# Attention, then two feed-forward stages: one unit's weights of each iteration copied into a rounded-format tile, transpositions moved to the end of the iteration two later

## The chip, the cores and the metric

The kernel runs on one core of a Trainium2 chip. That core has TensorE (PE in the profile; PEld is its weight load), VectorE (DVE), ScalarE (ACT), GpSimd (POOL) and SyncE (SP), which here only issues transfers. Each engine works through its own list of instructions in order and waits on semaphores that others raise. The metric is the device time of one execution in microseconds. The kernel before takes a median of 922.79 us over 3 runs (922.45 to 923.26).

## The reference

```python
def _attn_ref(q, k, v, tau):                      # q, k, v: 4 batches x 8 heads x 576 x 64
    scores = scale * np.matmul(q, k.transpose(0, 1, 3, 2))
    thresh = np.max(scores, axis=-1, keepdims=True) - tau
    scores = np.where(scores >= thresh, scores, -1000000000.0)
    scores = scores - np.max(scores, axis=-1, keepdims=True)
    attn = np.exp(scores)
    attn = attn / (np.sum(attn, axis=-1, keepdims=True) + 1e-09)
    return np.matmul(attn, v)
def reference(**kwargs):
    attn_out = _attn_ref(...)                      # -> x: 2304 tokens x 512
    x = _moe_ref(x=x, ...)                         # router, then one of 8 experts a token: relu(x w1) w2
    return _moe2_ref(x=x, ...)                     # h = x w_in; (h * sigmoid(1.702 h)) w_out
```

The change is in the attention. A row of the scores keeps only the entries within tau of its maximum; the exponentials of these, the weights, are summed and multiplied with the values.

## The kernel before, in words

Attention works on 16 pairs of heads of one batch. A pair is cut into 9 units: unit w = 2c + h (w under 8) has 128 queries of head h against all 576 keys, and unit 8 has the last 64 queries of both heads. That makes 144 units, taken two at a time in 72 iterations; an iteration's place in the pattern is k = it % 9, since nine iterations are two pairs of heads. Two tables indexed by k, AV and ROW, say how many items of value matmuls and of rows an iteration takes off their queues; AVL and ROWL do so for the last iterations. The loop is `run`.

In an iteration each engine is given, in this order of the program:

- scores (`qk`, L227), 6 matmuls a unit, 12 for unit 8. Queries and keys were each split into a rounded part and a rest (tiles qkh and qkl, format fp32r) by GpSimd (`split`, L149 to L151), so that three matmuls in that format give the product. They go into 4 banks that two units share by turns (ring).
- transpositions (`trans`, L313): four of 128 x 128 of the weights E of each of the two units of the iteration ahead, into one of three accumulators named tr, which rows and tails use too, in turn. ScalarE copies each accumulator into AT (L315, L317). In iterations k = 0, 2, 5, 7 come the transpositions of the last 64 keys, called tails (`trans_tails`, L331 to L335), copied to ATt (L340).
- per unit the negated maximum on VectorE (`max`, L255) and the exponential on ScalarE (`exp`, L261); behind these the copies of the transposed weights; then per unit the mask and sum on VectorE (`mask`, L285), which writes E (or ET for unit 8).
- value matmuls (`av_items`, L357), five items for each half of a pair, the last of them with the tails (L363) and a ScalarE copy to xT (L364).
- rows (`row_items`, L397): xT back to tokens by a matmul with G, which also gives the router's logits; copied by ScalarE to xr (L402), scaled by GpSimd (L405, L410), stored to DRAM by SP (L416).
- one or two items of GpSimd's splitting, and small steps of the router (`sides`; L658 adds a bias on VectorE).

F holds a pair's queries and keys, V its values; SP loads them two or three pairs ahead (L124, L128).

## Time and profile before

| what | us |
|---|---|
| median of 3 runs | 922.79 |
| profiled execution | 921.75 |
| its span | 920.0 |
| PE, DVE, ACT, POOL busy in the span | 898.1, 510.3, 445.2, 233.2 |
| attention, from the first scores to the first matmul of the next stage | 5.69 to 306.68 |
| nine iterations in the steady part (145.88 to 181.23) | 35.35 |

Busy time is what the instructions of an engine cover together. Matmuls overlap each other and their loads, so a mean duration of 280 ns for a small matmul isn't its share of the path; what a run of matmuls costs is read from the chain of waits, where pieces follow each other without overlap. The stretches of nine iterations below begin at the scores with k = 0.

### The profile page before, as it was taken

The numbers are of one execution on the slowest core, as the hardware profiler recorded it, in microseconds if no ns is written. First come the engines' busy times: TensorE is split into PE (matmuls) and PEld (weight loads), VectorE is DVE, ScalarE is ACT, GpSimd is POOL, SyncE is SP. The second block draws the span as 40 slices with busy tenths as digits, with TensorE's granted clock in tenths as the row PEclk, the third lists the DMA queues.
The fourth block names the chain that finished last, engine by engine and source line by source line (L and its number), as shares of the span: only waits on it lengthen the run. The fifth ranks groups of instructions, "written<-read, shape, count | busy, mean of one in ns | idle before, by whom it ended". The sixth has DMA issues, their size and how long they took to land.

```text
span 920.0 us, 14322 instructions
## 1 busy us (share of the span) xinstructions
PE 898.1 (98%) x5341; PEld 716.4 (78%) x5341; DVE 510.3 (55%) x1104; ACT 445.2 (48%) x787; POOL 233.2 (25%) x333
## 2 busy tenths in 40 slices
PE   9999999999999999999999999999999999999994
PEld 7677776776766788878889888888888888888894
DVE  7888889889787574678787588611111121111110
ACT  6777777777776533555545455422222222222221
POOL 7845655556544501010610000010001000100100
PEclk9999999999999999999999999999999999999997
DMA  7213432242102735465756153310001000100100
GB/s 257 73 46 122 140 128 72 71 131 74 36 9 76 239 103 187 142 230 178 229 183 231 68 184 117 112 46 12 24 12 46 7 12 7 46 0 1 46 1 26
DMA packets 53756, 85.67 MB, mean 93 GB/s; under 512 B 9300, under 2 KB 35058, under 8 KB 53682
## 3 DMA queue, kind: packets, MB, share of 16 engines
q1 hardware_dynamic: 50098, 74.63, 25.0%
q0 software_dynamic: 3312, 9.94, 3.3%
q8 instruction: 44, 0.72, 0.3%
q14 instruction: 30, 0.25, 0.1%
q10 hardware_dynamic: 272, 0.13, 0.0%
HBM read 67.57 MB, written 17.11 MB: 92 GB/s over the span
## 4 chain that ended last, share of the span: by engine, by line
PE 81%; DVE 7%; issue 6%; ACT 2%; DMA 2%; POOL 1%; SPq 0%; POOLq 0%; ACTq 0%
PE tr L1033 29%; PE sc L1058 19%; PE sc L1077 9%; PE sc L227 7%; PE av L357 6%; PE tr L313 6%; DVE E L285 3%; PE tr L397 2%; PE av L363 2%; DVE e L255 2%; ACT e L261 1%; DMA cv_raw<-in_moe_w_in_dram 1%; DMA xg<-y_first 1%; DVE bl L1303 1%; PE av L1005 1%
## 5 line engine op out<-in xcount | busy, mean ns | idle before, releaser
L1270 DVE TENSOR_TENSOR hl<-sg,hh 128x512 fp32r<-128x512 f32 (+1 forms) x80 | 51.1, 638 | 261.5 <-ACT hh L1268 259.1
L1267 ACT ACTIVATE sg<-tr 128x512 f32<-128x512 f32 (+1 forms) x80 | 44.3, 554 | 226.9 <-PE tr L1033 226.9
L261 ACT ACTIVATE e<-e,thr 128x576 f32<-128x576 f32 x144 | 109.6, 776 | 75.2 <-DVE e L255 74.6
L255 DVE TENSOR_SCALAR_CACHE_REDUCE e<-sc,taue 128x576 f32<-128x576 f32 x144 | 112.8, 815 | 33.7 <-PE sc L227 33.3
L1058 PE MATMUL sc<-wo_h,hh 128*128 128x512 f32 x288 | 112.2, 390 | 0.0
L1058 PE MATMUL sc<-wo_l,hh 128*128 128x512 f32 x288 | 112.2, 390 | 0.0
L1058 PE MATMUL sc<-wo_h,hl 128*128 128x512 f32 x288 | 112.0, 389 | 0.0
L285 DVE SCALAR_TENSOR_TENSOR E<-sc,thr,e 128x576 f32<-128x576 f32 x128 | 100.4, 813 | 5.1 <-ACT e L261 4.4
L1033 PE MATMUL tr<-xl,wi_h 128*128 128x512 f32 (+1 forms) x320 | 78.7, 368 | 0.0
L1033 PE MATMUL tr<-xh,wi_l 128*128 128x512 f32 (+1 forms) x320 | 78.7, 368 | 0.0
L1033 PE MATMUL tr<-xh,wi_h 128*128 128x512 f32 (+1 forms) x320 | 78.6, 368 | 0.0
L357 PE MATMUL av<-AT,V 128*64 128x288 f32 x512 | 77.3, 420 | 1.1 <-DVE ixs L933 0.6
L313 PE MATMUL tr<-ident,E 128*128 128x128 f32 x512 | 71.2, 279 | 0.0
L315 ACT COPY AT<-tr 128x512 f32<-128x512 f32 x128 | 68.2, 577 | 0.0
L1033 PEld LDWEIGHTS tr<-xh,wi_h 128*128 128x128 f32 x320 | 57.7, 188 | 11.1
L1033 PEld LDWEIGHTS tr<-xh,wi_l 128*128 128x128 f32 x320 | 56.9, 189 | 10.0
L1033 PEld LDWEIGHTS tr<-xl,wi_h 128*128 128x128 f32 x320 | 56.9, 189 | 9.9
L151 POOL TENSOR_TENSOR qkl<-F,qkh 128x640 fp32r<-128x640 f32 (+1 forms) x30 | 63.1, 2102 | 2.5
L313 PEld LDWEIGHTS tr<-ident,E 128*128 128x128 f32 x512 | 55.1, 141 | 10.3 <-issue 8.7
L1058 PEld LDWEIGHTS sc<-wo_h,hl 128*128 128x128 f32 x288 | 54.1, 188 | 11.3
L227 PE MATMUL sc<-qkh 64*128 64x288 f32 x320 | 57.0, 353 | 6.0 <-DVE E L285 4.2
L1058 PEld LDWEIGHTS sc<-wo_h,hh 128*128 128x128 f32 x288 | 54.1, 188 | 10.7
(262 smaller groups left out, 1578.2 us busy)
## 6 DMA issues: line engine op xcount, KB each, us to landing
F<-in_kq_dram SPq DMA_DIRECT2D x15, 896.0 KB
ra<-in_moe_w_dram SPq DMA_DIRECT2D x20, 512.0 KB
rb<-in_moe_w_dram SPq DMA_DIRECT2D x20, 512.0 KB
cv_raw<-in_moe_w_in_dram SPq DMA_DIRECT2D x16, 512.0 KB
cv_raw<-in_moe_w_out_dram SPq DMA_DIRECT2D x16, 512.0 KB
V<-in_vp_dram SPq DMA_DIRECT2D x16, 320.0 KB
x_dram<-xrow SPq DMA_DIRECT2D x72, 64.0 KB
y_rest<-blank SPq DMA_DIRECT2D x8, 256.0 KB
```

Source lines behind the costliest of these rows:

```text
L151: nc.gpsimd.tensor_sub(lo, x, hi.bitcast(F32))
L227: m = nc.tensor.matmul(self.banks[:, bank, 0:288], a[rs, q:q + 128], b[rs, k:k + 288], start=(n == 0), stop=(n == len(ops) - 1),).ins
L255: self.read(u, nc.vector.tensor_scalar(e, d["sc", w], self.taue[:, 0:1], 3.0e38, op0=ALU.add, op1=ALU.min, accum_out=thr))
L261: self.nc.scalar.activation(d["e", w], d["e", w], ACTF.Exp, bias=d["thr", w][:, 0:1], scale=-1.0)
L285: self.read(u, nc.vector.scalar_tensor_tensor(out=E.rearrange("p (a c) -> p a c", a=2), in0=d["sc", w], scalar=d["thr", w][:, 0:1], in1=d[ ...
L313: nc.tensor.transpose(tp[:, kc * 128:(kc + 1) * 128], E[:, k0 + kc * 128:k0 + (kc + 1) * 128], self.ident)
L315: return lambda: nc.scalar.copy(AT[:, h, :, c * 128:(c + 1) * 128], tp.rearrange("p (k c) -> p k c", k=4))
L357: nc.tensor.matmul(d["av"][h * 64:(h + 1) * 64, 0:288], d["V"][:, h, kc, :], d["AT"][:, h, kc, cols], start=(kc == 0), stop=False, skip_gr ...
L1033: nc.tensor.matmul(hps[:, 0:T], w[:, kd, :], blk[x][:, kd, 0:T], start=(i == 0), stop=(i == 11))
L1058: nc.tensor.matmul(y, h[:, cs], w, start=(f == 0 and i == 0), stop=(f == blk["nf"] - 1 and i == 2))
L1077: nc.tensor.matmul(blk["y"][d], w[:, ds], h[:, 0:T], start=(f == 0 and i == 0), stop=(f == last and i == 2))
L1270: return [upper, lambda: nc.vector.tensor_sub(hl, sg, hh.bitcast(F32))]
```

## The change

Each iteration's first unit gets a copy of its 512 columns of weights: `lay` has SP copy E into a tile R of the rounded format (bits are kept, the tile's type is fp32r), behind that unit's mask. `trans` transposes R with an identity of that type if there is an R, and E as before otherwise. Transpositions no longer follow the scores of the next iteration; they stand at the end of the iteration two later, behind value matmuls and rows, and their ScalarE copies stand there too. ATt is taken from its pool with the first tails instead of with the first transposition. E has five buffers instead of four, F two instead of three.

`split` takes queries by head, so it has three steps in place of two, and the loads of F come in two halves that are queued among these steps. Stores of rows to DRAM are collected and issued behind the masks of the next iteration. The tables AV, ROW, AVL, ROWL and FILL (matmuls on the identity in the first iterations) have other numbers. The router's small sum always takes a tr accumulator.

```diff
--- before.py
+++ after.py
@@ -25,12 +25,12 @@
 UPP = 9
 PJ = 9
 QW, KW = 1280, 640
-AV = (2, 2, 3, 3, 2, 2, 3, 2, 1)
+AV = (1, 3, 2, 3, 2, 2, 3, 2, 2)
 TURNS = ((0, 1), (2, 3))
 TAILS = {2: -1, 5: -2, 7: -2, 0: -1}
 IT_LAST = (NPAIR - HP) * UPP // 2
-AVL = (2, 2, 3, 2, 3, 2, 3, 2, 1, 2, 2, 3, 3, 2, 2, 3, 3, 2, 5)
-ROWL = (0, 1, 0, 1, 1, 1, 1, 1, 1, 0, 0, 0, 0, 1, 0, 1, 0, 1, 0)
+AVL = (1, 3, 2, 3, 2, 2, 3, 2, 2, 1, 3, 2, 3, 2, 2, 3, 2, 2, 1, 5)
+ROWL = (2, 0, 1, 0, 0, 1, 1, 1, 1, 1, 0, 0, 0, 0, 0, 0, 1, 0, 1, 1)
 NS0 = 7
 CA = (0, 1, 2, 2, 2, 2, 2, 2, 2, 2, 2, 2, 2, 2, 2, 2)
 CB = (0, 0, 0, 1, 0, 1, 0, 1, 0, 1, 0, 1, 0, 0, 0, 0)
@@ -40,12 +40,12 @@
 NBW = 6
 F0 = (0, 1, 0)
 NROW = 2
-FILL = (14, 12, 12, 12, 4)
+FILL = (14, 16, 12, 12, 6)
 SN = 1
 SD = (1, 2, 2, 2, 1)
 TAU_MAX = 104.0
 W_TOP = (1.875 - 2.0 ** -23) * 2.0 ** -96
-ROW = (0, 1, 0, 1, 1, 0, 1, 0, 1)
+ROW = (2, 0, 1, 0, 0, 0, 0, 1, 1)
 
 class Attention:
 
@@ -74,8 +74,9 @@
         self.banks = P("a_sc", 1, space=PSUM).tile([128, 4, 512], F32, name="sc")
         Q = lambda name, bufs: late_ctx.enter_context(tc.tile_pool(name=name, bufs=bufs, side="right"))
         cst = P("a_const", 1)
-        self.fp = P("a_f", 3)
-        self.ep = P("a_e", 4)
+        self.fp = P("a_f", 2)
+        self.er = P("a_er", 3)
+        self.ep = P("a_e", 5)
         self.ex = P("a_exp", 3)
         self.et = P("a_et", 2)
         self.sm = P("a_small", 4)
@@ -89,6 +90,8 @@
         self.rp = Q("a_rows", 2)
         self.rw = Q("a_xrow", 6)
 
+        self.idr = cst.tile([128, 128], F32R, name="idr")
+        nc.gpsimd.tensor_copy(self.idr, ident)
         self.cq = cst.tile([128, 1], F32, name="cq")
         self.taue = cst.tile([128, 1], F32, name="taue")
         self.tau = tau
@@ -118,10 +121,13 @@
                 )
 
 
-    def load(self, p):
-        d = self.st[p] = {}
-        d["F"] = F = self.fp.tile([128, KW + 2 * S], F32, name="F")
-        self.nc.sync.dma_start(F, self.kq[p])
+    def load(self, p, parts=(0, 1)):
+        if 0 in parts:
+            self.st[p] = {"F": self.fp.tile([128, KW + 2 * S], F32, name="F")}
+        n = (KW + 2 * S) // 2
+        for i in parts:
+            cs = slice(i * n, (i + 1) * n)
+            self.nc.sync.dma_start(self.st[p]["F"][:, cs], self.kq[p][:, cs])
 
     def load_v(self, p):
         V = self.vp.tile([128, 640], F32, name="V")
@@ -142,7 +148,9 @@
     def split(self, p, i):
 
         nc = self.nc
-        x, (hi, lo) = (self.keys, self.queries)[i](p)
+        x, (hi, lo) = self.queries(p) if i else self.keys(p)
+        if i:
+            x, hi, lo = (t[:, i - 1] for t in (x, hi, lo))
         if i == 0 and p == 1:
             nc.scalar.activation(x, x, ACTF.Copy, scale=self.cq[:, 0:1])
         elif i == 0:
@@ -296,6 +304,16 @@
             ]
 
 
+    def lay(self, u):
+
+        p, w = divmod(u, UPP)
+        d = self.st[p]
+        c, h = divmod(w, 2)
+        E = d["E", 4] if w == 8 else d["E", c][:, h]
+        k0 = 64 if w < 8 and h == 1 else 0
+        d["R", w] = self.er.tile([128, 512], F32R, name="R")
+        self.nc.sync.dma_start(d["R", w].bitcast(F32), E[:, k0:k0 + 512])
+
     def trans(self, u):
 
         nc = self.nc
@@ -304,13 +322,17 @@
         c, h = divmod(w, 2)
         if w == 0:
             d["AT"] = self.at.tile([128, 2, 4, S], F32, name="AT")
-            d["ATt"] = self.at.tile([128, S], F32, name="ATt")
-        AT, ATt = d["AT"], d["ATt"]
+        AT = d["AT"]
         tp = self.ps_tr.tile([128, 512], F32, name="tr")
+        R = d.pop(("R", w), None)
         E = d["E", 4] if w == 8 else d["E", c][:, h]
         k0 = 64 if w < 8 and h == 1 else 0
         for kc in range(4):
-            nc.tensor.transpose(tp[:, kc * 128:(kc + 1) * 128], E[:, k0 + kc * 128:k0 + (kc + 1) * 128], self.ident)
+            cs = slice(kc * 128, (kc + 1) * 128)
+            if R is not None:
+                nc.tensor.transpose(tp[:, cs].bitcast(F32R), R[:, cs], self.idr)
+            else:
+                nc.tensor.transpose(tp[:, cs], E[:, k0 + kc * 128:k0 + (kc + 1) * 128], self.ident)
         if w < 8:
             return lambda: nc.scalar.copy(
                 AT[:, h, :, c * 128:(c + 1) * 128], tp.rearrange("p (k c) -> p k c", k=4))
@@ -323,6 +345,8 @@
         nc = self.nc
         p, w = divmod(u, UPP)
         d = self.st[p]
+        if w == 3:
+            d["ATt"] = self.at.tile([128, S], F32, name="ATt")
         ATt = d["ATt"]
         c0 = 0 if w == 3 else 2
         n = 256
@@ -413,7 +437,8 @@
                 rr.unsqueeze(3).broadcast_to([w, 2, 2, 64]),
             )
             for u in range(2 if kc < 4 else 1):
-                nc.sync.dma_start(xd[b, 2 * kc + u][:, hh * 256:(hh + 1) * 256], xrow[u * 64:(u + 1) * 64, :])
+                self.stores.append(lambda u=u: nc.sync.dma_start(
+                    xd[b, 2 * kc + u][:, hh * 256:(hh + 1) * 256], xrow[u * 64:(u + 1) * 64, :]))
             if hh == 1 and kc == 4:
                 items, gate = self.router.gate_items(b, lgt)
                 self.side.extend([None] * (1 if b == B - 2 else NROW) + items + self.router.after_batch(b, gate))
@@ -428,27 +453,29 @@
         rest = self.first()
         self.load_v(0)
         self.load_v(1)
-        self.load(2)
-        self.poolq = []
+        self.poolq, self.stores = [], []
         self.avq, self.rowq, self.side = avq, rowq, side = [], [], []
         side += [None] * NS0 + [self.gate_setup, *self.router.setup_items(self.setup), *self.extra]
         it = done = 0
         while done < NU:
             last = it >= IT_LAST
             us = [u for u in (2 * it, 2 * it + 1) if u < NU]
-            ts = [u for u in (2 * it - 2, 2 * it - 1) if 0 <= u < NU]
+            ts = [u for u in (2 * it - 4, 2 * it - 3) if 0 <= u < NU]
             starts = [u // UPP for u in us if u % UPP == 0]
             for p in starts:
-                if p + 3 < NPAIR:
-                    self.load(p + 3)
-                if p + 2 < NPAIR:
+                if 0 < p < NPAIR - 2:
                     self.load_v(p + 2)
                 for n in range(1 if p == 0 else p + 2, min(p + 3, NPAIR)):
                     self.poolq += [lambda n=n, i=i: self.split(n, i) for i in range(2)]
+                    if n + 2 < NPAIR:
+                        self.poolq += [lambda n=n: (self.split(n, 2), self.load(n + 2, (0,)))]
+                        self.poolq += [lambda n=n: self.load(n + 2, (1,))]
+                    else:
+                        self.poolq += [lambda n=n: self.split(n, 2)]
             k = it % 9
             for u in us:
                 self.qk(u)
-            copies = [self.trans(u) for u in ts]
+            copies = []
             if it > 1 and k in TAILS:
                 copies.append(self.trans_tails(2 * it + TAILS[k]))
             for i in range(2):
@@ -461,12 +488,18 @@
                 c()
             while rest:
                 rest.pop(0)()
+            if it == 0:
+                self.load(2)
+                self.load_v(2)
             if self.norm:
                 self.norm.pop(0)()
             for i, u in enumerate(us):
                 self.mask(u)
+                if i == 0:
+                    self.lay(u)
                 if last:
                     self.sides(SD[i + 2], False)
+            self.store()
             if it < len(FILL) and FILL[it]:
                 warm = self.ps_av.tile([128, 512], F32, name="av")
                 for _ in range(FILL[it]):
@@ -477,6 +510,8 @@
             while m and rowq:
                 rowq.pop(0)()
                 m -= 1
+            for c in [self.trans(u) for u in ts]:
+                c()
             n = 1 if it else 2
             while n and self.poolq:
                 self.poolq.pop(0)()
@@ -489,12 +524,18 @@
                     avq += self.av_items(p, w // 8)
             it += 1
 
+    def store(self):
+
+        while self.stores:
+            self.stores.pop(0)()
+
     def tail(self, n):
 
         for _ in range(n):
             for q in (self.avq, self.rowq):
                 if q:
                     q.pop(0)()
+                    self.store()
                     break
         return bool(self.avq or self.rowq)
 
@@ -918,7 +959,7 @@
 
         def sum_up(c0, c1):
             if c0 == 0:
-                t["ip"] = self.ps_av.tile([128, 512], F32, name="av") if first else self.ps_tr.tile([128, 512], F32, name="tr")
+                t["ip"] = self.ps_tr.tile([128, 512], F32, name="tr")
             for c in range(c0, c1):
                 nc.tensor.matmul(
                     t["ip"][:, 0:2 * nh], OL[:, c, :], R[:, c].rearrange("p i h -> p (i h)"),
```

TensorE in an iteration with k = 0 (the 36th, counted from 0), before, from behind its scores to the first scores of the next; E and ET are weights, tr the accumulators, G the matrix that turns rows:

```order
L313 MATMUL tr<-ident,E 128x128 [waits Activation_49]
L313 MATMUL tr<-ident,E 128x128 x3
L313 MATMUL tr<-ident,ET 128x128 [waits Activation_49]
L313 MATMUL tr<-ident,ET 128x128 x3
L331 MATMUL tr<-ident,ET 128x128 [waits Activation_49]
L332 MATMUL tr<-ident,ET 64x128
L335 MATMUL tr<-ident,E 128x128 x2
L357 MATMUL av<-AT,V 64x288 x2
L363 MATMUL av<-ATt,V 128x288
L227 MATMUL sc<-qkh_139 128x288 [waits DVE_49]
```

The same iteration after, from behind its scores:

```order
L355 MATMUL tr<-ident,ET 128x128 [waits Activation_49]
L356 MATMUL tr<-ident,ET 64x128
L359 MATMUL tr<-ident,E 128x128 x2
L387 MATMUL av<-ATt,V 128x288
L421 MATMUL tr<-G,xT 128x144 [waits Activation_49]
L421 MATMUL tr<-G,xT 128x144
L421 MATMUL tr<-G,xT 128x144 [waits Activation_49]
L421 MATMUL tr<-G,xT 128x144
L333 MATMUL tr<-idr,R 128x128 [waits DMAHW0_49,Activation_49]
L333 MATMUL tr<-idr,R 128x128 x3
L335 MATMUL tr<-ident,E 128x128 [waits Activation_49]
L335 MATMUL tr<-ident,E 128x128 x3
```

The eight transpositions moved behind the tails, the tail value (L387) and now two rows (L421); the value matmuls on AT are in other iterations, and the last four transpositions wait for ScalarE.

ScalarE in the same iteration, before; e is the exponential, AT and ATt the transposed weights:

```order
L261 ACTIVATE e<-e,thr 128x576 [waits DVE_49,Activation_49] x2
L315 COPY AT<-tr 128x4x128 [waits PE_49]
L317 COPY AT<-tr 128x4x2x64 [waits PE_49]
L340 COPY ATt<-tr 128x320 [waits PE_49]
L364 COPY xT<-av 128x288 [waits PE_49]
L261 ACTIVATE e<-e,thr 128x576 [waits DVE_49,Activation_49] x2
```

After:

```order
L269 ACTIVATE e<-e,thr 128x576 [waits DVE_49,Activation_49] x2
L364 COPY ATt<-tr 128x320 [waits PE_49]
L388 COPY xT<-av 128x288 [waits PE_49]
L426 COPY xr<-tr 128x288 [waits PE_49,Pool_49]
L426 COPY xr<-tr 128x288 [waits PE_49,Activation_49,Pool_49]
L337 COPY AT<-tr 128x4x128 [waits PE_49] x2
L269 ACTIVATE e<-e,thr 128x576 [waits DVE_49]
```

The copies of AT moved from right behind the exponentials to the end of the iteration, behind the copies of ATt, xT and the rows.

## Rows read from the trace of the kernel before

**Rows 1.** Stretches of nine iterations: from:to, length; busy (instructions) by engine; clock; DMA.
```profile
5.69:38.50 32.81, 30.88 (x277) 23.99 (x277) 28.73 (x72) 23.45 (x41) 29.26 (x32) 1.00 0.39 149
38.50:73.75 35.25, 34.71 (x290) 24.16 (x290) 30.09 (x81) 26.09 (x48) 19.08 (x32) 1.00 0.26 82
...
109.36:145.88 36.52, 35.33 (x297) 25.14 (x296) 31.53 (x80) 26.29 (x50) 19.88 (x21) 1.00 0.30 96
145.88:181.23 35.35, 35.30 (x298) 25.17 (x298) 30.25 (x83) 26.51 (x51) 20.42 (x24) 1.00 0.29 89
...
254.93:288.33 33.40, 32.16 (x278) 22.45 (x277) 30.24 (x88) 24.20 (x48) 17.21 (x57) 1.00 0.06 12
288.33:306.68 18.35, 17.20 (x131) 12.35 (x129) 9.41 (x20) 10.76 (x23) 9.20 (x17) 1.00 0.65 199
```

**Rows 2.** One iteration, k = 7, in the same view.
```profile
173.83:177.18 3.35, 3.35 (x31) 2.38 (x31) 2.48 (x7) 2.22 (x5) 3.19 (x6) 1.00 0.00 0
```

**Rows 3.** Chain of waits, 145.8 to 181.3: start us, us, what.
```profile
161.72 1.39 PE sc L227 x18
...
164.12 0.64 PE av L357 x4
...
165.93 0.98 PE sc L227 x12
166.91 1.02 PE tr L313 x8
...
168.16 0.22 PE tr L335 x2
168.38 1.12 PE av L357 x8
...
172.73 0.68 PE av L363 x2
173.41 0.49 PE tr L397 x4
...
176.27 1.57 DVE E L285 x4
...
180.61 0.69 PE tr L397 x4
```

**Rows 4.** Groups by line and shape: x count, busy us, mean ns, idle before.
```profile
L1033 PE MATMUL tr<-xl,wi_h 128*128 128x512 f32 x256 | 68.4, 389 | 0.0
...
L1033 PEld LDWEIGHTS tr<-xh,wi_h 128*128 128x128 f32 x320 | 57.7, 188 | 11.1
...
L1033 PE MATMUL tr<-xl,wi_h 128*128 128x256 f32 x64 | 10.3, 283 | 0.0
```

**Rows 5.** Timeline, ScalarE, in k = 0: start us, us, what.
```profile
147.51 1.51 ACT L261 ACTIVATE e<-e,thr 128x576 f32<-128x576 f32 x2 [0.91 <-DVE e L255]
...
149.40 0.59 ACT L317 COPY AT<-tr 128x512 f32<-128x512 f32 x1
149.87 0.44 ACT L340 COPY ATt<-tr 128x320 f32<-128x320 f32 x1
150.19 0.42 ACT L364 COPY xT<-av 128x288 f32<-128x288 f32 x1
```

**Rows 6.** Timeline, all engines, 241.3 to 243; in brackets idle time and releaser.
```profile
241.43 0.56 ACT L317 COPY AT<-tr 128x512 f32<-128x512 f32 x1
...
242.05 0.54 PEld L397 LDWEIGHTS tr<-G,xT 128*128 128x128 f32 x4 [0.54 <-ACT AT L317]
```

**Rows 7.** Timeline of GpSimd and VectorE around 137; durations of L658.
```profile
136.57 2.65 POOL L151 TENSOR_TENSOR qkl<-F,qkh 128x1152 fp32r<-128x1152 f32 x1
...
137.09 2.18 DVE L658 TENSOR_TENSOR L<-L,bias 128x40 f32<-128x40 f32 x1
...
L658 DVE TENSOR_TENSOR L<-L,bias x4: 189/1192/2184, 137.1 to 315.0; 128x40 f32<-128x40 f32 x4
```

**Rows 8.** Half a microsecond of the transfer of V, in stretches.
```profile
59.50:60.00 0.50, 0.50 (x6) 0.50 (x7) 0.50 (x3) 0.00 (x0) 0.50 (x2) 1.00 0.82 302
```

## The prediction

> **What bounds the kernel now.** I read the stretches of nine iterations first (they show how much of the span the attention takes and whether it is even), then the chain of waits inside one such stretch, then the rows of single operations on it. Attention runs from 5.69 us to the first matmul of the second stage at 306.68 us; the steady stretch takes 35.35 us, and TensorE is busy for 35.30 of them, VectorE for 30.25, ScalarE for 26.51, at a granted clock of 1.00, the 2.4 GHz level [rows 1]. So in the steady state TensorE is the bound. One iteration of the nine isn't: the seventh (k = 7, counting k from 0) takes 3.35 us [rows 2], and the chain there leaves TensorE for two masks, 1.57 us of VectorE, before the next scores [rows 3]. 3.35 is therefore my floor for an iteration: scores, maxima, exponentials, masks and the scores again run in a ring over the same banks, and no change to transpositions shortens that.
>
> The prices on TensorE's path come from the chain [rows 3]: scores 0.98 (1.39 with a unit of tails), eight transpositions 1.02, two tail transpositions 0.22 (so 0.11 each, and 1.02 is 8 x 0.11 with 0.14 of edge), value matmuls 0.64 for one item and 1.12 for two (0.16 + 0.48 an item), the tail value 0.68, a row 0.49 behind a tail value and 0.69 behind value matmuls.
>
> **The change part by part.**
>
> *The format.* Half of the transpositions, 4 of 8 in an iteration and 288 in all, now read a rounded-format tile. No row shows that operation. Lower bound: the same format costs 389 ns at 512 columns and 283 at 256, so 0.053 us per 128 columns when nothing but columns counts [rows 4]. Upper bound with no harm: F32's 0.11. Beyond that it could be worse, since a weight load in the rounded format lasts 188 ns by itself [rows 4] and might not hide behind a short matmul; taken wholly unhidden that is 0.19. The nearest row is the scores: 12 matmuls of that format, each with its own load of 128 columns, in 0.98 us, or 0.082 each [rows 3]. I take 0.08. The difference of 0.03 is worth 36 x 0.03 = 1.1 us in nine iterations, if nothing else ends later.
>
> A rule of the Trainium skill speaks against this, TensorE: Matmul & The Clock Gate, section LDWEIGHTS (loading the stationary operand): a load takes the number of columns over 1.2 in ns, whatever the rest. For 128 columns that would be an estimated 107 ns in either format, and the format would gain nothing (the third case below). The 0.98 for 12 loads of 128 columns speaks against it, though those loads fill only half of the rows each.
>
> *The order.* The group of eight stands behind the value matmuls and rows now, in front of the next scores, instead of behind the scores. By the same edges it costs 4 x 0.08 + 4 x 0.11 + 0.14 = 0.90 behind value matmuls and 0.76 behind a row or tail value, which as the chain shows begin without the edge. Four of the nine are of the first kind, five of the second: 4 x 0.90 + 5 x 0.76 = 7.4 against 9 x 1.02 = 9.2. Together with one more 0.16 saved (eight starts of value matmuls, not nine), TensorE's work falls by 2.0 us per nine iterations, format included.
>
> *The waits that it adds.* Three accumulators serve all of these transpositions and the rows in turn. In an iteration with tails the tails take one, a row another, and the fourth allocation needs the first again. It is freed by ScalarE's copy, and ScalarE makes the copies only behind both exponentials, which end at 147.51 + 1.51 = 149.02, 3.14 us after the scores of that iteration began, at 145.88 [rows 1, 5]. That TensorE does wait so is in the trace once already: a row's load sat 0.54 us for the copy of AT and began 0.06 behind its end, 241.43 + 0.56 = 241.99 [rows 6]. A copy begins about 0.12 before the one ahead of it ends (149.40 + 0.59 against 149.87).
> - k = 0: work 0.98 + 0.44 + 0.68 + 0.49 + about 0.45 + 0.76 = 3.80. But the last four transpositions wait for the first row's copy, which stands behind ATt (0.44) and xT (0.42) on ScalarE: 3.14 + 0.44 + 0.42 + about 0.41 - 3 x 0.12 = 4.05, then 0.06 and 4 x 0.11 = 4.55, with an edge 4.65. Cost 0.85.
> - k = 2 and 7: work 3.77 each; the last four wait for the ATt copy, about 3.14 + 0.44 - 0.12 + 0.06 + 0.44 = 3.96, with an edge 4.0. Cost 0.25 each.
> - k = 4: work 1.39 + 0.64 + 0.68 + 0.76 = 3.47, under the ring, 3.35 + 0.41 for the longer scores = 3.7. Cost 0.2.
> - k = 5: work 3.44, with the ring of the iteration ahead about 3.75. Cost 0.3.
> - k = 1 and 3: 0.98 + 1.60 + 0.90 = 3.48; k = 6: 3.54; k = 8: 3.96. No wait.
> That is 4.65 + 2 x 4.0 + 3.7 + 3.75 + 6.96 + 3.54 + 3.96 = 34.56; I take 34.85, since the ring makes each edge of 0.03 to 0.05 late that I left out. So of the 2.0 us, 1.5 is given back, and 0.5 is left of each steady stretch.
>
> *Two stretches with a blocked VectorE.* At 137.09 a small addition takes 2.18 us while GpSimd's subtraction of 1152 columns (2.65 us) is under way; its fastest case takes 0.19 [rows 7]. The stretch around it takes 36.52, 1.17 more than the steady one [rows 1], and a later one is like it. Now the queries are split by head, so the subtraction is 576 wide, an estimated 1.4 us, and by its place should end ahead of that addition. I take -1.0 for each of the two; at worst 0.
>
> *Start and end.* The first stretch is GpSimd's (29.26 busy of 32.81 [rows 1]): 0. In the second no rows stand in k = 0 and 2 yet, so those waits are absent and it gains nearly the whole 2.0: -1.9. The eighth (33.40) runs by the end's own tables: I take -1.0. The drain of 18.35 [rows 1] gets one iteration more: the last units are transposed two later, and their copy must land first. That adds the group and the copy's time that the remaining values don't cover: +2.5 (0.76 at least, 4 at most).
>
> *Transfers.* 72 copies of 256 KB on SP's queue. The transfer of V reached 302 GB/s [rows 8], so a copy alone needs an estimated 1 us and its fixed time; it is issued behind the first mask, some 3.3 us into an iteration, and read some 7 us later. What stands behind it on SP, the stores and loads, has more time than that. In steady state 0. At the start, copies stand behind the loads of the third pair: +0.5 (0 to 2).
>
> The sum: 0 - 1.9 - 5 x 0.5 - 2 x 1.0 - 1.0 + 2.5 + 0.5 = -4.4 us. The profiled execution took 921.75, of which 920.0 span, and lies 1.04 under the median 922.79; the difference carries over, so the forecast is 922.8 - 4.4 = 918.4.
>
> **The rivals.** They hang on the price of a rounded transposition, since all else is the same. 288 of them, and about half of a change in price arrives, because k = 0, 2, 4, 5 and 7 end on waits.
> - *The price is the lower bound, 0.053.* The columns alone count and the load hides, as for 512 columns. 288 x 0.027 = 7.8, half 3.9: 914.5. For it: every long matmul of that format hides its 188 ns. Against: the scores' 0.082.
> - *The format gains nothing, 0.11.* 288 x 0.03 = 8.6, half 4.3: 922.7. For it: a load of 188 ns is no shorter than any F32 load. The gain of order and of GpSimd is then eaten by the waits at k = 0, 2, 7 and by the drain.
> - *Slower: the load is not hidden.* The place is the four rounded transpositions of each iteration; it decides above 0.11 each. At 0.14 nothing is absorbed any longer: 922.7 + 288 x 0.03 = 931; with 0.125, 927. For it: 188 ns by itself and a moving side of 128 columns only. Against: the scores.
> - *The copies are late.* If a copy takes beyond 7 us from the mask, TensorE stands in every iteration: 0.1 us is 7 us in all, 925. Against: 89 GB/s in the steady stretch [rows 1] against 302 reached.
>
> **How the numbers follow.** Forecast 0.42 (own range 916.4 to 920.8, from the bounds of the drain and of the blocked stretches); lower price 0.22; no gain 0.17; load not hidden 0.10; late copies 0.09. The range 914.5 to 926 leaves out half of the last two and the far end of the second. A measurement of this kernel tells 0.2%, 1.8 us, from no change: faster than that is the forecast, less a tenth of it, and the second case, 0.60; the third gives most of the 0.2 of no change; slower 0.20.
>
> **What would show it.** Right: rounded transpositions 0.08 apart; a wait of TensorE for a ScalarE copy of a row in every k = 0 and of ATt in k = 2 and 7; steady stretches of 34.6 to 35.1; the router's addition back near 0.2; a drain of 20 to 21. Wrong: waits on the copy's DMA outside the first iterations and the end; a steady stretch under 34.3 (the price is lower, or the waits are not there) or above 35.4.

## The result and the profile after

The changed kernel took 927.39 us (median of 4 runs, 926.05 to 928.01) against 922.62 for the kernel before (4 runs): 1.0051 times as long, 95% interval 1.0039 to 1.0063. So it is 4.8 us slower, where 4.4 us faster was forecast and 926 was the upper end of the range.

The busy times on the page of the profiled execution, whose span is 926.2 us:

```profile
PE 896.1 (97%) x5347; PEld 711.3 (77%) x5347; DVE 511.6 (55%) x1104; ACT 449.4 (49%) x787; POOL 239.4 (26%) x364
```

TensorE does less (896.1 us instead of 898.1) in a span that is 6.2 us longer; the time is in waits. The stretches of nine iterations again, which answer to [rows 1]; the last line is the drain to the first matmul of the next stage. The last two lines are divided one iteration later than in [rows 1], so only their sum can be compared:

```profile
5.68:39.07 33.39, 31.04 (x279) 23.71 (x278) 29.13 (x73) 23.03 (x39) 29.65 (x42) 1.00 0.63 213
39.07:74.26 35.19, 33.42 (x285) 22.84 (x285) 31.19 (x81) 25.97 (x47) 17.68 (x29) 1.00 0.43 141
74.26:110.20 35.94, 34.82 (x297) 24.25 (x297) 29.32 (x77) 26.90 (x50) 22.45 (x28) 1.00 0.65 214
110.20:146.33 36.13, 35.16 (x297) 24.38 (x296) 30.34 (x81) 27.03 (x50) 20.56 (x26) 1.00 0.59 191
146.33:183.32 36.99, 35.34 (x297) 24.39 (x296) 32.08 (x82) 27.17 (x51) 21.36 (x31) 1.00 0.48 149
183.32:219.58 36.26, 35.24 (x297) 24.34 (x297) 31.49 (x84) 27.02 (x50) 20.71 (x27) 1.00 0.48 153
219.58:257.30 37.72, 35.85 (x305) 25.33 (x305) 30.09 (x85) 27.85 (x53) 23.17 (x36) 1.00 0.33 105
257.30:293.83 36.53, 34.10 (x303) 23.37 (x302) 32.56 (x95) 26.16 (x50) 17.50 (x57) 1.00 0.23 77
293.83:311.39 17.56, 15.62 (x111) 12.00 (x111) 6.94 (x14) 10.37 (x23) 10.57 (x19) 1.00 0.75 233
```

That stage begins at 311.39 instead of 306.68, 4.7 us later. Against the steps of the prediction: the first stretch was forecast at 32.8 (and 0.5 for the start) and took 33.4; the second at 33.3 and took 35.2; the five behind it, 181.2 us before, at 176.7 and took 183.0; the last stretch and the drain together, 51.8 before, at 53.3 and took 54.1. Nearly the whole miss, 8.2 of 9.1 us, is in the second to seventh stretch.

One of these, iteration by iteration, k = 0 to 8 (length, then busy time by engine):

```profile
110.20:114.90 4.70, 4.32 (x37) 3.51 (x36) 3.53 (x11) 3.86 (x9) 1.26 (x4) 1.00 0.93 276
114.90:118.71 3.81, 3.59 (x34) 2.36 (x34) 3.04 (x8) 2.89 (x6) 3.66 (x6) 1.00 0.79 290
118.71:123.29 4.58, 4.50 (x33) 2.75 (x34) 3.90 (x11) 3.25 (x7) 3.85 (x5) 1.00 0.35 106
123.29:126.81 3.52, 3.52 (x33) 2.35 (x32) 2.81 (x8) 2.58 (x5) 3.28 (x5) 1.00 0.38 130
126.81:130.62 3.81, 3.54 (x33) 2.56 (x33) 3.01 (x9) 2.50 (x6) 3.66 (x4) 1.00 0.88 268
130.62:134.50 3.88, 3.88 (x33) 2.53 (x33) 3.71 (x10) 2.76 (x7) 3.72 (x4) 1.00 0.60 210
134.50:138.32 3.82, 3.81 (x31) 2.46 (x30) 3.65 (x10) 3.21 (x7) 0.21 (x1) 1.00 0.20 73
138.32:142.37 4.05, 4.05 (x36) 2.85 (x35) 3.46 (x12) 3.14 (x7) 0.22 (x2) 1.00 0.58 178
142.37:146.33 3.96, 3.96 (x39) 3.00 (x38) 3.21 (x8) 2.84 (x6) 0.71 (x3) 1.00 0.57 182
```

| k | 0 | 1 | 2 | 3 | 4 | 5 | 6 | 7 | 8 |
|---|---|---|---|---|---|---|---|---|---|
| forecast | 4.65 | 3.48 | 4.0 | 3.48 | 3.7 | 3.75 | 3.54 | 4.0 | 3.96 |
| measured | 4.70 | 3.81 | 4.58 | 3.52 | 3.81 | 3.88 | 3.82 | 4.05 | 3.96 |

Six of nine are within 0.13. k = 1, 2 and 6 are off by 0.3 to 0.6, and VectorE is behind all three. For k = 1 and 2, the timeline from 115.89 to 119.45:

```profile
115.89 1.89 POOL L157 TENSOR_SCALAR F<-F,cq 128x640 f32<-128x640 f32 x1
...
117.19 0.60 DVE L301 COPY rs<-rsT 64x2 f32<-64x2 f32 x1
...
118.71 0.40 PE L235 MATMUL sc<-qkh 64*128 64x288 f32 x2 [0.22 <-DVE E L293]
...
119.44 0.19 PEld L235 LDWEIGHTS sc<-qkh 64*128 64x128 f32 x2 [0.31 <-DVE E L293]
```

The copy of 64 x 2 numbers at L301, a step of the normalisation that `run` places in front of the masks, took 0.60 us; it began while GpSimd scaled 640 columns (115.89 + 1.89 = 117.78) and ended at 117.79. Undisturbed it takes 0.16, and both masks behind it came late by the difference; the next scores waited 0.22 us for the first mask, and those of the second unit 0.31 for the second. The light iteration had no TensorE work left to cover that. In k = 6 the second unit's scores waited 0.24 for the second mask of k = 5, whose maxima had begun behind a router step of 0.78 us (L697).

The price of the rounded transposition, though, is as forecast. Chain of waits (start, us, what), behind value matmuls, then behind a tail value:

```profile
133.64 0.47 PE tr L333 x4
134.11 0.46 PE tr L335 x4
...
137.63 0.30 PE tr L333 x4
137.93 0.47 PE tr L335 x4
...
139.40 0.37 PE tr L359 x2
```

Four rounded transpositions take 0.30 us, 0.075 each (forecast 0.08), and the four in F32 behind them 0.46. The group costs 0.93 behind value matmuls and 0.76 to 0.77 behind a tail value (forecast 0.90 and 0.76). What I left out is the edge of 0.15 that moved to the tails: 0.37 for two tail transpositions right behind scores, where they were 0.22 behind other transpositions [rows 3].

The wait that was forecast for k = 0 is there, for the copy of ATt and then the row's:

```profile
113.71 0.53 PE L333 MATMUL tr<-idr,R 128*128 128x128 f32 x4 [0.31 <-ACT ATt L364]
...
114.31 0.42 PEld L335 LDWEIGHTS tr<-ident,E 128*128 128x128 f32 x4 [0.21 <-ACT xr L426]
```

And the router's addition of [rows 7] is short again, as forecast, min/median/max:

```profile
L699 DVE TENSOR_TENSOR L<-L,bias x4: 193/195/202, 135.0 to 319.7; 128x40 f32<-128x40 f32 x4
```

But other small steps now meet GpSimd's. VectorE and GpSimd around 157:

```profile
157.08 1.40 POOL L159 TENSOR_TENSOR qkl<-F,qkh 128x576 fp32r<-128x576 f32 x1
...
157.09 1.42 DVE L302 TENSOR_SCALAR r<-rs 128x20 f32<-128x20 f32 x1
```

L302, 20 numbers a partition, lasts 1.42 us, to the end of GpSimd's subtraction (157.08 + 1.40 = 158.48). The shorter subtraction did not end these meetings; it moved them. The Trainium skill, SBUF — State Buffer, section "SBUF: two separate sides", says that the port pair which VectorE and GpSimd share is "an exclusive lock, not a bandwidth split". The ends of the two agree within 0.03 us here.

This meeting cost little: k = 2 and 3 of its stretch take 4.58 and 3.68, where the stretch above has 4.58 and 3.52. Another one, of a router step in k = 4 of the same stretch, cost more; its durations (min/median/max), and k = 4 and 5:

```profile
L719 DVE TENSOR_TENSOR oh<-v,valid x4: 194/200/1403, 167.5 to 321.1; 128x40 bf16<-128x40 f32 x4
...
163.17:168.82 5.65, 5.37 (x51) 3.86 (x50) 4.82 (x13) 3.50 (x7) 5.08 (x6) 1.00 0.89 282
168.82:171.42 2.60, 2.11 (x18) 1.24 (x18) 2.43 (x8) 1.70 (x3) 2.40 (x5) 1.00 0.26 93
```

Together these two take 8.25, 0.56 more than the 3.81 and 3.88 above. In the second stretch L667, 1.5 us at 58.3, does the same: k = 4 and 5 take 5.93 and 2.43 there.

### The profile page after: what moved, and what is told of

Read it like the earlier page. It is cut to its first block, busy times and chain, and to the rows that moved or that the text cites. A ratio compares the mean times of both kernels' runs of the same rounds, so it can differ in the third digit from the quotient of the medians.

```text
span 926.2 us, 14670 instructions
## 1 busy us (share of the span) xinstructions
PE 896.1 (97%) x5347; PEld 711.3 (77%) x5347; DVE 511.6 (55%) x1104; ACT 449.4 (49%) x787; POOL 239.4 (26%) x364
## 4 chain that ended last, share of the span: by engine, by line
PE 73%; issue 8%; DVE 6%; DMA 5%; POOL 4%; ACT 3%; SPq 0%; POOLq 0%; ACTq 0%; DVEq 0%
PE tr L1074 27%; PE sc L1099 19%; PE sc L1118 7%; PE sc L235 6%; PE av L381 5%; PE tr L335 2%; DMA cv_raw<-in_moe_w_in_dram 2%; PE tr L421 2%; DVE E L293 2%; PE tr L333 2%; DVE e L263 1%; POOL qkl L159 1%; DMA R<-E 1%; PE av L387 1%; ACT e L269 1%
## 5 line engine op out<-in xcount | busy, mean ns | idle before, releaser
L337 ACT COPY AT<-tr 128x512 f32<-128x512 f32 x128 | 70.4, 593 | 2.1 <-PE tr L333 1.4
L159 POOL TENSOR_TENSOR qkl<-F,qkh 128x576 fp32r<-128x576 f32 (+1 forms) x45 | 65.8, 1462 | 3.7
L1099 PEld LDWEIGHTS sc<-wo_h,hl 128*128 128x128 f32 x288 | 54.1, 188 | 11.4
L1099 PEld LDWEIGHTS sc<-wo_h,hh 128*128 128x128 f32 x288 | 54.1, 188 | 10.6
L1099 PEld LDWEIGHTS sc<-wo_l,hh 128*128 128x128 f32 x288 | 54.1, 188 | 10.6
L1363 POOL DMA_INDIRECT out_dram<-cv_e,iscA x4 | 4.0, 993 | 223.5 <-ACT cv_e L1433 222.9
```

What stands on the lines that cost most here:

```text
L159: nc.gpsimd.tensor_sub(lo, x, hi.bitcast(F32))
L337: return lambda: nc.scalar.copy(AT[:, h, :, c * 128:(c + 1) * 128], tp.rearrange("p (k c) -> p k c", k=4))
L1099: nc.tensor.matmul(y, h[:, cs], w, start=(f == 0 and i == 0), stop=(f == blk["nf"] - 1 and i == 2))
```

## The experiments

Theories, as they came. A: the transpositions' new place costs, since short iterations end on VectorE's ring. B: the copies' traffic costs. C: the finer split of the queries and its loads costs. D: the tables AV and ROW cost: an iteration lasts as long as the longer of TensorE's pieces and VectorE's ring, and the new tables make heavy iterations (two rows beside tails in k = 0) and light ones (3.5). E: a small VectorE step that meets a GpSimd step lasts until its end, so what counts is where the two meet. F: the finer split costs wherever it stands. All times are medians; the kernel before had 922.6 to 923.1 beside them.

**No rounded format, copies kept.**
```diff
-        R = d.pop(("R", w), None)
+        d.pop(("R", w), None)
+        R = None
```


> The changed kernel, but every transposition reads E in F32; the copies into R are still made and read by nobody. Theory A (the format is worth 0.03 us a transposition, and the new place loses it again because short iterations end on VectorE's ring): steady stretches longer by about half of 36 x 0.035 us, so 4 to 5 us more than the changed kernel's 927.4, 931 to 932. Theory B (the copies' traffic is what costs): the format's worth is lost here as well and the traffic stays, 931 or more. By itself it measures the format.

Measured 928.61. By the medians the format is worth 1.2 us here, not 4 to 5; the intervals of the two ratios to the kernel before (1.0060 and 1.0051) overlap, so even 1.2 is at the edge of what these runs tell apart.

**Neither format nor copies**: also without the call of `lay`.

> The changed kernel without the copies and without the rounded format. Theory A: as the run with unread copies, within 1.5 us (930 to 933). Theory B: the copies cost 5 us or more in all, so 927 or less, at least 4 us under the run with unread copies.

Measured 928.80, the same as with unread copies and under theory A's range too. Theory B falls.

**Transpositions behind the scores.**
```diff
-            copies = []
+            copies = [self.trans(u) for u in ts]
...
-            for c in [self.trans(u) for u in ts]:
-                c()
```


> The changed kernel, copies and format kept, with the eight transpositions back right behind the scores (still those of two iterations ahead) and their ScalarE copies back behind the exponentials. Theory A: the waits for ATt and the row's copy in k = 0, 2, 7 go, and 0.9 us of transpositions stand between scores and the rest again: 917 to 922 with these tables. Theory B, and theory C (the finer split of the queries and its loads cost): nothing changes by the place, 926 to 929.

Measured 933.26: worse, so theory A finds nothing for it here. But this run doesn't show the place alone: with the copies kept, the place by the scores also reads R one iteration's work earlier, and TensorE waits for copies (see the run with the tables of before below). Two of the four runs took 930.74 and 931.26 at a granted clock of 0.995 over the span, the other two 935.26 and 936.95 at 0.991 and 0.992. The F32 runs below take the copies out.

**Normalisation in k = 0.**
```diff
-            if self.norm:
+            while self.norm and k == 0:
                 self.norm.pop(0)()
```


> The changed kernel with the four small VectorE steps of the normalisation all in k = 0, where VectorE stands idle 1.2 us, instead of one each in k = 0 to 3. Theory A: k = 1 falls from 3.85 to about 3.5 and k = 2 from 4.59 to 4.25, some 0.7 us in each of seven stretches, 922 to 923. Theories B and C: 927 as before.

Measured 925.45, 1.9 us better. k = 1 and 2 of the stretch shown above:

```profile
115.08:118.61 3.53, 3.53 (x34) 2.36 (x33) 2.72 (x7) 2.61 (x5) 3.46 (x5) 1.00 0.87 319
118.61:122.99 4.38, 4.38 (x34) 2.75 (x33) 3.60 (x10) 3.45 (x8) 4.03 (x6) 1.00 0.34 104
```

k = 1 falls from 3.81 to 3.53 and k = 2 from 4.58 to 4.38. The mechanism is right at its place; it is 0.5 us a stretch and not the 0.7 expected, and the second stretch gives 0.6 back (35.77 against 35.19).

**The tables of before**, at the new place, with copies, format and split as changed.
```diff
-AV = (1, 3, 2, 3, 2, 2, 3, 2, 2)
+AV = (2, 2, 3, 3, 2, 2, 3, 2, 1)
-ROW = (2, 0, 1, 0, 0, 0, 0, 1, 1)
+ROW = (0, 1, 0, 1, 1, 0, 1, 0, 1)
```
AVL and ROWL go back too, with one more entry for the longer end.

> The changed kernel with the tables AV and ROW of the kernel before (and the end's tables of before, one iteration longer); place, copies, format and split as changed. Theory D (an iteration lasts as long as the longer of TensorE's own pieces and VectorE's ring, and the new tables split the pieces into light and heavy iterations, with rows in iterations with tails): no row stands in k = 0, 2, 5, 7 now, the heaviest iteration falls from 4.7 to about 4.1, steady stretch 34.4 instead of 36.2, total 915 to 919. Theory A (the place itself costs): 925 to 928. Theory C (the finer split and its loads): 925 to 928.

Measured 918.02, ratio to before 0.9951 (0.9934 to 0.9967). The stretch that answers to the one above, and its k = 0 and 2:

```profile
108.28:142.78 34.50, 34.42 (x298) 24.32 (x298) 30.12 (x80) 26.55 (x51) 20.57 (x25) 1.00 0.59 188
108.28:112.27 3.99, 3.91 (x31) 2.62 (x31) 3.88 (x11) 3.35 (x8) 3.74 (x5) 1.00 0.93 286
...
115.83:119.90 4.07, 4.07 (x33) 2.66 (x32) 3.87 (x10) 3.26 (x7) 3.91 (x6) 1.00 0.29 105
```

36.13 has become 34.50, k = 0 has gone from 4.70 to 3.99 and k = 2 from 4.58 to 4.07. Theory D stands: the tables cost 9.4 us, twice what the whole change lost. What TensorE's matmuls waited for between 10 and 290 us (us in all, times, longest), in the changed kernel and then in this run, shows where:

```profile
PE sc L235 <- DVE E L293: 5.0, 11, 1.1
PE tr L333 <- ACT ATt L364: 2.1, 5, 0.6
...
PE sc L235 <- DVE E L293: 2.0, 6, 0.5
```

Waits for masks, those of ET (2.4 and 0.8) included, fall from 7.4 to 2.8 us, and those for the copy of ATt, 3.0 with 0.9 at L335, are gone. Rarer meetings of VectorE and GpSimd aren't the reason: between 30 and 300 us the four normalisation steps last 11.6 us in all in the changed kernel and 10.7 here, the router's L707 and L719 2.4 there and 4.6 here.

**The tables of before, transpositions behind the scores.**

> As the run before in this list, with the transpositions and their copies behind the scores again. Theory D: the pieces of the kernel before, less 0.14 in each iteration that TensorE bounds: steady stretch about 34.2, 914 to 918. Theory C: 922 or more.

Measured 937.15, far off. The longest wait for a copy that had not landed, and the iteration that it stands in (k = 2 of the third stretch; the clock is the third number from the end):

```profile
89.88 0.50 PE L333 MATMUL tr<-idr,R 128*128 128x128 f32 x4 [2.53 <-DMA R<-E]
...
86.30:94.10 7.80, 5.27 (x33) 2.95 (x33) 3.21 (x9) 3.26 (x6) 6.86 (x7) 0.82 1.02 388
```

There are eight such waits, 10.4 us in all. Behind the longest one the granted clock fell, so that the iteration has 0.82 on average and not 1.00; over the span of this execution it is 0.986, where the changed kernel has 0.995. A copy takes a median of 2.3 us from issue to landing. The one of the longest wait was issued at 88.07, behind a load of F at 86.85. At the end of the iteration, with the same tables, TensorE waits for a copy only twice, 0.9 us in all.

**The same without format and copies.**

> As the second run in this list, all transpositions in F32 and no copies: the kernel before, one iteration later and with the queries split by head. Theory D: as the kernel before plus the longer drain, 922 to 925, and 6 to 9 us above the second run, since there the price of a transposition arrives. Theory C: the finer split costs alone, 927 or more.

Measured 926.25. As no copy can be late here, this is the place by the scores without the copies; the end of the iteration, also in F32 and with these tables, takes 920.52 (below). So the new place gains 5.7 us. In the profiled executions the last stretch begins 4.0 us earlier at the new place (251.12 against 255.09); the rest is one iteration near the end, of which more below.

**Queries split in one step**: `split` takes both heads at step 1, and step 2 returns at once.

> The changed kernel with the queries of both heads split in one step again, as before (1152 columns), the third step of the queue only loading. Theory C: at least 3 us faster, 924 or less. Theory D: no gain; VectorE's small steps meet a longer GpSimd step, 927 to 930.

Measured 924.96, a gain of 2.4 us: against theory D's expectation, and for theory C as far as this run goes, though short of its 3 us. The gain stands in the stretches with the meetings above: the second takes 34.18 (35.19 with the finer split) and the fifth 35.93 (36.99), while the third and fourth stay at 35.94 and 36.13; L667 lasts 0.25 us here, and L719 at most 0.39. The run with the tables of before, further down, turns the sign round.

**Three changes together**: tables of before, one split, normalisation two steps each in k = 2 and 3.

> Three gains together: the changed kernel with the tables of before (918.0 alone), the queries split in one step (2.4 us better on the changed kernel), and the four normalisation steps two each in k = 2 and 3, which TensorE bounds. If the three add: 913 to 916. If the last two were gains only at the places where the new tables left TensorE waiting: 917 to 919.

Measured 929.64, over both expectations: they don't add, they undo each other. VectorE and GpSimd in a k = 2:

```profile
118.78 2.65 POOL L159 TENSOR_TENSOR qkl<-F,qkh 128x1152 fp32r<-128x1152 f32 x1
...
119.03 2.42 DVE L300 COPY rs<-rsT 64x2 f32<-64x2 f32 x1
...
121.46 0.16 DVE L301 COPY rs<-rsT 64x2 f32<-64x2 f32 x1
```

The first normalisation step, a copy of 64 x 2 numbers, now meets the longer subtraction and lasts 2.42 us.

**The tables of before, F32, no copies.**

> The changed kernel with the tables of before, all transpositions in F32, no copies. Theory D: with even iterations most of the format's 0.035 us x 288 = 10 us arrives, so 923 to 927, against 918.0. If the format is absorbed here too, as it was with the new tables (1.2 us): 919 to 920.

Measured 920.52, so the format is worth 2.5 us with even iterations, twice as much as with the new tables and a quarter of what 288 x 0.035 makes; theory D's 923 to 927 falls. Chain of waits of this run, two groups of eight, the first behind a tail value, the second behind value matmuls:

```profile
111.53 0.87 PE tr L336 x8
...
131.04 1.02 PE tr L336 x8
```

and of the run with the format and these tables, at the same places:

```profile
111.59 0.29 PE tr L333 x4
111.88 0.46 PE tr L335 x4
...
130.75 0.47 PE tr L333 x4
131.22 0.46 PE tr L335 x4
```

0.87 against 0.75, and 1.02 against 0.93: about 0.1 us an iteration and not 0.14. The four in F32 behind rounded ones take 0.46, not half of 0.87, and the edge behind value matmuls is 0.18 (0.47 - 0.29) and not 0.15. Of the 0.9 that this makes in nine iterations 0.55 arrives (35.05 against 34.50), and the first stretch is 0.7 longer with the copies (33.37 against 32.69; with the new tables and copies that nobody reads, 33.66 against 32.94).

**The new tables by the scores, F32.**

> The new tables with the transpositions behind the scores, all in F32, no copies; to be held against the 926.3 of the same kernel with the tables of before. Theory D: the tables cost by themselves, at this place too: 930 to 934. If they cost only in connection with the transpositions at the end: 925 to 928.

Measured 932.11, 5.9 us above the same with the tables of before. Part of this is the clock: two of the four runs took 934.14 and 935.88 at a granted clock of 0.993 and 0.991, the other two 929.48 and 930.08 at 0.996 and 0.995. In the profiled execution the clock fell with a wait of 3.0 us for GpSimd that ended at 327.8, after the attention; up to the last stretch the new tables cost 5.0 us (260.12 against 255.09). The tables cost at either place.

**Only ROW of before.**

> The changed kernel with only the table ROW of before (0, 1, 0, 1, 1, 0, 1, 0, 1), so that no row stands in an iteration with tails; AV and the end's tables as changed. Theory D: k = 0 falls from 4.7 to 3.4 to 3.7 and k = 2 from 4.6 to about 3.6, while k = 1, 3, 4, 6 get a row each: steady stretch 34.0 to 34.8, total 916 to 920. If the table of value matmuls is what costs: 924 or more.

Measured 920.79, just over theory D's range. A stretch and its k = 0:

```profile
108.27:143.27 35.00, 34.27 (x297) 24.33 (x296) 30.07 (x80) 26.70 (x50) 20.62 (x26) 1.00 0.59 186
108.27:111.59 3.32, 2.88 (x28) 2.33 (x27) 2.71 (x10) 2.47 (x5) 3.25 (x4) 1.00 0.99 291
```

6.6 of the 9.4 us are the rows alone; the other 2.8, AV and the end's tables, were not taken apart. k = 0 is light now and ends on VectorE's ring (3.32), and k = 1, with a row, takes 4.38.

**The tables of before, queries split in one step.**

> The changed kernel with the tables of before and the queries split in one step; the normalisation steps where they were. Theory E (a small VectorE step that meets GpSimd's subtraction lasts until its end, so only the meeting counts, not the size): what it gives depends on whether k = 0 to 3 and the router's steps meet the longer subtraction; the normalisation of k = 2 does by the trace of the run with both edits, so 918 to 922. Theory F (the finer split costs wherever it stands): 915 to 916.5.

Measured 923.43, 5.4 us worse than with the finer split. The fourth stretch takes 36.80 (34.50 with the finer split); its k = 2:

```profile
115.86:121.26 5.40, 4.16 (x33) 2.66 (x33) 5.21 (x10) 4.01 (x8) 4.50 (x4) 1.00 0.23 84
```

In that k = 2 L302 met the subtraction again and lasted 2.43 us. With even tables the finer split gains; theory F is out. Theory E's mechanism stands, though 923.43 is over its 922, and its "not the size" does not: a step that meets the longer subtraction waits to the longer end. L300, L302 and L699 last 15.5 us in all between 30 and 300 us, against 7.8 with the finer split.

**Three normalisation steps on GpSimd**, with the tables of before: `nc.gpsimd` in the first three lines that `mask` adds to `norm`.

> The changed kernel with the tables of before and three of the four normalisation steps on GpSimd instead of VectorE, so that they can't meet GpSimd's subtraction. Theory E: the calls of 0.6 us in k = 1 and their like go from VectorE's ring: 0.1 to 0.4 us in each of seven stretches, 915.5 to 917.5. If those meetings cost nothing with these tables: 918 to 919.

Measured 917.48 (917.07 to 917.98), the lowest median; it is 0.5 under the run without it (917.69 to 918.94), but the two ranges overlap, so that these steps cost anything with these tables is not shown.

Put together, the eight combinations of place, tables and format (copies go with the format), with the start of the last stretch of attention in the profiled execution in brackets:

| us | tables of before | new tables |
|---|---|---|
| behind the scores, F32 | 926.25 (255.09) | 932.11 (260.12) |
| behind the scores, rounded | 937.15 (262.71) | 933.26 (266.79) |
| end of the iteration, F32 | 920.52 (251.12) | 928.80 (258.15) |
| end of the iteration, rounded | 918.02 (249.23) | 927.39 (257.30) |

From the kernel before to the changed one the medians add up so: 922.6, and 3.6 for all that isn't place, tables or format, less 5.7 for the place, less 2.5 for the format with its copies, and 9.4 for the tables, makes 927.4. In F32, where no copy can be late, the new place is ahead with either set of tables, by 5.7 and 3.3 us (4.0 and 2.0 up to the last stretch), so theory A falls.

## Why the prediction was wrong

- *What bounds the kernel*: right for the kernel before, and it misled for the one after. I took TensorE as the bound with one iteration as an exception; the new tables left TensorE waiting in others, k = 1 and 6 (for masks) and k = 4 (for GpSimd's split) among them. The ring's sum for k = 4, 3.35 + 0.41, is 3.76 and was put down as 3.7; it took 3.81.
- *The format*: 0.08 forecast, 0.075 measured. The likeliest case was the right one of the rivals. That half of it arrives was wrong: 1.2 us of 10 at most with the new tables, 2.5 with those of before.
- *The order*: the group's 0.90 and 0.76 were 0.93 and 0.76. The 2.0 us saved were less by the edge that moved to the tails, 0.15 in each of four iterations.
- *The waits that it adds*: **this step failed**. Its k = 0 and 7 were right to 0.05. But I gave VectorE's ring as a floor of 3.35 without the small steps that run inside it, and took each iteration by itself, where a late mask makes the second unit's scores of the next iteration wait (0.31 in k = 2). I allowed 0.3 us a stretch for that. The third to seventh stretch took 0.8, 1.1, 2.1, 1.0 and 1.2 more than my steps for each (0.5 less than before, 1.5 less in the fourth and sixth). I also priced the new tables only as they stood and never against those of before at the same place; the sum over the pieces would have shown that rows beside tails put waits into k = 0 and 2 for which no other iteration gets shorter than the ring. The runs with the tables of before show it: 9.4 us, with TensorE's waits for masks at 2.8 instead of 7.4 and none for ATt.
- *Two stretches with a blocked VectorE*: the cause and the size were right for these two. In the fourth, k = 6 and 7 took 6.43 and 2.51 before and take 3.83 and 4.05 now, 1.06 less; the gain is hidden under what the waits add. What I left out is that the finer split makes more and shorter GpSimd steps, which other small steps meet: L301, L302, L667 and L719. Those that fall into iterations without cover cost, 0.56 in the fifth stretch, and I didn't look for them.
- *Start and end*: the second stretch, -1.9 forecast, gained 0.06; 1.0 of the miss goes with the meeting of L667 at 58.3, as the run with one split shows (34.18). The last stretch and the drain, +1.5 together, were +2.3.
- *Transfers*: right at this place. The rival of late copies had the right point to watch and the wrong kernel: it decides when the transpositions stand by the scores.
- *The slower rival* was an unhidden weight load of 188 ns; at these transpositions the load lasts 140 ns and four follow each other 0.075 us apart. There was a slower mechanism, and it was another; 926 as the upper end was 1.4 us too low.

What the runs leave open: with the tables of before, in F32, the place by the scores costs 3.6 us more than the kernel before itself (926.25 against 922.6), from which it differs by one iteration of delay, the finer split, the loads and the accumulator of the router's small sum. No run takes these apart, but the traces say where it is. Up to the last stretch the two are even (255.09 against 254.93), so delay, split and loads cost next to nothing there. The next to last iteration with scores takes 6.51 us, where the kernel before takes 3.48 (284.85 to 288.33, at a clock of 1.00):

```profile
284.83:291.34 6.51, 4.60 (x37) 2.50 (x36) 3.50 (x13) 2.75 (x5) 2.06 (x3) 0.74 0.08 20
287.77 0.56 PE L961 MATMUL tr<-R,OL 128*128 128x16 bf16 x15 [1.91 <-ACT AT L338]
```

L961 is the router's small sum, which now takes a tr accumulator and waits 1.91 us for a copy of AT; behind that wait the clock fell. At the new place, in F32 and with these tables, the same iteration takes 3.08, so about half of the 5.7 us that the new place gains comes from it. Whether the old accumulator would save them was not tried.

## What to carry to other kernels

Before pricing a faster instruction, write for each step of the cycle the longer of two sums, the busy engine's and the ring's with all its small steps, and carry lateness into the next step; a saving in a step that is already at the ring is worth nothing. Work that can be put anywhere (rows here) belongs in the steps with cover, and a table that places it should be priced against the old one by itself. When two engines block each other, shortening one instruction moves the meeting; count the meetings anew.

## What the runs showed of the hardware

A VectorE copy of 64 x 2 numbers took 0.16 us alone and 2.42 us when it began 0.25 us into a GpSimd subtraction of 2.65 us, while VectorE's maxima and masks, which read the accumulators, never passed 0.83 us. A rounded transposition of 128 x 128 runs at 0.075 us where F32 takes 0.11, though both weight loads last about the same in the trace (140 and 141 ns); four of one kind and four of the other gain 0.1 and not 0.14. TensorE's granted clock was 1.00, the 2.4 GHz level, throughout the attention of the changed kernel, and it fell for a while to 0.50, the 1.2 GHz level, with or behind single waits of 1.91, 2.53 and 3.0 us in three of the runs; twelve value matmuls behind the first of these took 3.15 us, where twelve in the changed kernel took 1.68. Not each wait did that: one of 2.14 us before 53.1 us, in the run with the new tables behind the scores, left it at 1.00.
